# Down-sampled attention and a gated feed-forward layer in one kernel: w_out by seven products in the middle stage, in a written step order

## The chip, the core and the metric

The kernel runs on one core of one Trainium2 chip. The metric is the device time of one execution in microseconds (us). A core has TensorE (matrix products, into PSUM, eight banks of 512 float32 per partition), VectorE, ScalarE, GpSimd and SyncE. In the profile they are PE (PEld for its weight loads), DVE, ACT, POOL and SP. Each works through its own queue in order, and they wait for each other by semaphores. DMAs are issued from the queues of GpSimd, SyncE and ScalarE.

## The reference

Two layers follow each other. The first is attention over 8 batches of 8 heads, 576 positions of width 64: a coarse attention on q, k and v averaged over groups of four positions, its output repeated four times, plus a local one in which each position sees the three neighbours on either side. The second takes the result as 4608 tokens of width 512 through a gated layer of width 1536.

```python
out_d = sm_attn(q_d, k_d, v_d)                  # q, k, v averaged over 4 positions
out_up = np.repeat(out_d, factor, axis=2)
mask = np.abs(pos[:, None] - pos[None, :]) < factor
...
out_local = np.matmul(attn, v)                  # softmax inside the mask
x = (out_up + out_local) as tokens x 512
gate = np.maximum(x @ w_gate, 0.0)
val = x @ w_val
return gate * val @ w_out
```

## The kernel before

All five engines follow the order in which the program is written (`manual_schedule`); nothing is moved by a planner at build time, so the order of the calls is the order of each queue.

The attention is done by head pairs, 32 of them (`hp`), four to a batch. The feed-forward layer is done by chunks of 512 tokens, nine of them (`c`), in four slots each. Slot `s` belongs to chunk `s // 4` and works on head pair `s + 4`: the attention runs four pairs ahead. So slots 0 to 27 hold both, slots 28 to 35 hold the feed-forward layer alone (the tail), and four filling steps come before slot 0.

A slot of the middle stage (from slot 8; `emit_slot`) does this:

- `emit_h` three times: gate and value product of one 128-wide piece of the 1536, each four matmuls of 128x512 (`emit_h_mm`, line 516) into a pair of banks. ScalarE takes the relu of the gate half (line 531), VectorE multiplies it with the value half into `gT` (line 532, the "gate"). Pairs 0 and 1 (banks 0 to 3) take turns.
- `emit_y`: the w_out product of 128 tokens of the chunk before, twelve matmuls of 128x512 (line 541), a copy by ScalarE (line 549) and an output DMA from ScalarE's queue.
- `emit_s1`, written inside `emit_y` after its first two matmuls: the scores of the pair (lines 314 and 325) into banks 4 to 7, two exponentials and one for the coarse scores by ScalarE (lines 334 and 343), two mask products by VectorE (line 337).
- `emit_pool`: VectorE sums q and k of the next pair over four positions (line 234), from the transposed copy `qkT` that a transposing DMA on SP's queue (`emit_qkT`) made two slots earlier.
- `emit_s2w`: sums and denominators of the attention (lines 459 and 467), again into banks 4 to 7, a logarithm of each head's denominators (line 477), an exponential for the inverse (line 480), two products by VectorE (`xn`, line 483), and `emit_xsum` (line 442), which adds the repeated coarse part and writes `xT`, what the feed-forward products read.
- GpSimd issues the loads four pairs ahead: q and k (line 195) into `qk16`, v (line 220) into `vw`, rings of seven; v once more in another layout into `v4` (line 222), a ring of five. From this it pools v in two adds, `emit_v2` (line 280) and `emit_v1` (line 286), into `vd`, a ring of three.

The tail does w_out by units of 256 tokens (`Unit`): a 2x2 blocked product by seven products in place of eight, of six matmuls of 128x256 each (line 603). Four sums of the token side (`s1` to `s4`, line 597) and four differences of the weights (`emit_wt`, line 572, made in slots 24 to 27) are formed by VectorE. The products `p1` to `p7` accumulate into three PSUM regions `a`, `b`, `d`. Between them ScalarE copies `a` into `m1`, `m2`, `m3`, and VectorE adds these to `b` or `d` for the output blocks. In the tail `a`, `b` and `d` have a bank each.

Of the kernel before, what the change touches and what calls it, by code (L numbers as in the profile page):

```python
# [14 lines left out]
ET = mybir.EngineType  # L15

# [41 lines left out]
def kernel(  # L58
# [27 lines left out]
    VS = 8  # L86
# [23 lines left out]
    def ring(n, shape, dtype, name):  # L110
# [3 lines left out]
    NV4 = 5  # L114
# [12 lines left out]
    xo = ring(3, [96, NB + 2, 128], FP16, "xo_")  # L127
    rden = ring(2, [128, 2, 360], FP32, "rden_")
    xn = ring(2, [128, 2, 360], FP16, "xn_")
# [7 lines left out]
    wt = [  # L137
        t.rearrange("p i c -> p (i c)").rearrange("p (j d) -> p j d", d=256) for t in qkfull[0:4]
# [38 lines left out]
    def emit_load_qk(hp):  # L177
        r = hp % NL
        b, off = head_off(hp)
        for src, dst in ((q, qk16[r][:, 0, :]), (k, qk16[r][:, 1, :])):  # L180
            if hp == 0 and src is q:
                nc.sync.dma_start(
                    q32.rearrange("p (n d) -> p n d", d=64),
                    _dap(src, off, [[D, 96], [NQ * D, 2 * NB], [1, D]]),
                )
                nc.scalar.copy(out=dst, in_=q32)
            elif hp < NTP:
                nc.gpsimd.dma_start(
                    dst.rearrange("p (n d) -> p n d", d=64),
                    _dap(src, off, [[D, 96], [NQ * D, 2 * NB], [1, D]]),  # L190
                )
            else:
                dv = dst.rearrange("p (j h d) -> p j h d", h=2, d=64)
                for hh in range(2):
                    nc.gpsimd.dma_start(  # L195
                        dv[:, :, hh, :],
                        _dap(src, off + hh * S * D, [[D, 96], [NQ * D, NB], [1, D]]),
                    )

    def emit_load_v(hp):  # L200
# [18 lines left out]
        else:  # L219
            nc.gpsimd.dma_start(t, _dap(v, base, [[D, WK], [NQ * D, n], [1, D]]))  # L220
        if hp >= NVP:
# [87 lines left out]
    def emit_s1(hp, p0):  # L309
# [22 lines left out]
        for g in range(2):  # L332
            o = ee[r2][:, :, 288 * g : 288 * g + 288]
            nc.scalar.activation(  # L334
                out=o, in_=ps[0:WK, p0 + 2 * g : p0 + 2 * g + 2, 0:288], func=AF.Exp, scale=scale
            )
            nc.vector.tensor_tensor(  # L337
                out=o,
                in0=o,
                in1=_sap(masks_sb, (0, WK), 288 * g, [[0, 2], [1, 288]]),  # L340
                op=ALU.mult,
            )
        nc.scalar.activation(  # L343
            out=ed[r2][:, :, 0 : 2 * SD].rearrange("p h (c t) -> p c h t", c=2),
# [3 lines left out]
        )  # L348

# [43 lines left out]
    def emit_s2t(hp, between):  # L393
        r2 = hp % 2
        e, d = ee[r2], ed[r2]
        for g in range(2):
            for hh in range(2):
                nc.tensor.matmul(  # L398
                    out=ps[64 * hh : 64 * hh + 64, 4 + g, 0:288],
# [5 lines left out]
            for c in range(2):  # L405
                for hh in range(2):
                    nc.tensor.matmul(
                        out=ps[64 * hh : 64 * hh + 64, 4 + g, 288:360],
# [5 lines left out]
        for g in range(2):  # L414
            for j in range(3):
                for hh in range(2):
                    nc.tensor.matmul(
                        out=ps[64 * hh : 64 * hh + 64, 2 + g, NQ * j : NQ * j + NQ],
# [5 lines left out]
            for c in range(2):  # L424
                for hh in range(2):
                    nc.tensor.matmul(
                        out=ps[64 * hh : 64 * hh + 64, 2 + g, 288:360],
# [5 lines left out]
        r, x = rden[r2], xn[r2]  # L433
        nc.scalar.activation(out=r, in_=ps[:, 4:6, 0:360], func=AF.Ln)
        between()
        nc.scalar.activation(out=r, in_=r, func=AF.Exp, scale=-1.0)
        nc.vector.tensor_tensor(out=x, in0=ps[:, 2:4, 0:360], in1=r, op=ALU.mult)
        emit_xsum(hp)

    def emit_xsum(hp):  # L440
        b, kk, x = hp // NPB, hp % NPB, xn[hp % 2]
# [6 lines left out]

    def emit_s2w(hp):
        r2 = hp % 2  # L450
        vflat = vw[hp % NL].rearrange("p b c -> p (b c)")
        e, d = ee[r2], ed[r2]
        for hh in range(2):
            for g in range(2):
                bank = 4 + 2 * hh + g
                for j in range(3):
                    lo = 288 * g + NQ * j
                    v0 = 128 * (NB * hh + 3 * g + j) - 64 * hh
                    nc.tensor.matmul(  # L459
                        out=ps[:, bank, NQ * j : NQ * j + NQ],  # L460
                        lhsT=vflat[:, v0 : v0 + 128],
                        rhs=e[:, hh, lo : lo + NQ],
                        start=True,
                        stop=True,
                    )
                for c in range(2):
                    nc.tensor.matmul(  # L467
                        out=ps[:, bank, 288:360],
                        lhsT=vd[hp % 3][:, c, 64 * hh : 64 * hh + 128],
                        rhs=d[:, hh, c * SD + 72 * g : c * SD + 72 * g + 72],  # L470
                        start=(c == 0),
                        stop=(c == 1),
                    )
        r, x = rden[r2], xn[r2]
        for hh in range(2):
            lo, de = 64 * hh, 64 - 64 * hh
            nc.scalar.activation(  # L477
                out=r[lo : lo + 64], in_=ps[de : de + 64, 4 + 2 * hh : 6 + 2 * hh, 0:360], func=AF.Ln
            )
        nc.scalar.activation(out=r, in_=r, func=AF.Exp, scale=-1.0)  # L480
        for hh in range(2):
            lo = 64 * hh
            nc.vector.tensor_tensor(  # L483
                out=x[lo : lo + 64],
                in0=ps[lo : lo + 64, 4 + 2 * hh : 6 + 2 * hh, 0:360],
                in1=r[lo : lo + 64],
                op=ALU.mult,
            )
# [35 lines left out]
    def emit_h(c, jj, pp, parts=((0, range(4)), (1, range(4)))):  # L524
        h1, h2 = pair(pp)[:, 0, :], pair(pp)[:, 1, :]
# [3 lines left out]
        def gate():  # L529
            r1 = ffn.tile([128, TCH], FP16, name="r1", tag="r1")  # L530
            nc.scalar.activation(out=r1, in_=h1, func=AF.Relu)  # L531
            nc.vector.tensor_tensor(out=gT[c % 2][:, jj, :], in0=r1, in1=h2, op=ALU.mult)  # L532

        return gate
# [33 lines left out]
    def emit_wt(i):  # L568
        (b11, b12), (b21, b22) = halves
        t1, t2, t3, t4 = wt  # L570
        o, a, b = ((t1, b12, b11), (t2, b22, t1), (t3, b22, b12), (t4, b21, t2))[i]
        nc.vector.tensor_tensor(out=o, in0=a, in1=b, op=ALU.subtract)

    class Unit:


        def __init__(self, c, u, banks):
            self.c, self.u = c, u
            self.a, self.b, self.d = (ps[:, k, 0:256] for k in banks)
            self.s1, self.s2, self.s3, self.s4 = sa[u]  # L580
            self.m1, self.m2, self.m3 = sums[u]
# [19 lines left out]
        def mm(self, out, left, right, first):  # L601
            for i in range(NK):
# [3 lines left out]
                    rhs=right[:, i, :],  # L606
# [5 lines left out]
        def p1(self):  # L612
# [3 lines left out]
            self.mm(self.a, self.x[0][0], halves[0][0], True)  # L616
            nc.scalar.copy(out=self.m1, in_=self.a)

        def p2(self):
            self.mm(self.d, self.x[0][1], halves[1][0], True)  # L620
            nc.vector.tensor_tensor(out=self.y[0][:, 0:256], in0=self.d, in1=self.m1, op=ALU.add)
            self.out(0, 0)

        def p6(self):
            self.mm(self.a, self.s2, wt[1], False)
            nc.scalar.copy(out=self.m2, in_=self.a)
# [3 lines left out]

        def p7(self):
            self.mm(self.a, self.s3, wt[2], False)
            nc.scalar.copy(out=self.m3, in_=self.a)
# [3 lines left out]
        def p4(self):  # L637
            self.mm(self.a, self.x[1][1], wt[3], False)
# [223 lines left out]
```

The softmax here doesn't subtract the row's maximum and nothing guards it: scores larger than these inputs give would overflow.

## Time and profile before

| | before |
|---|---|
| median of 8 runs | 353.87 us (353.14 to 354.64) |
| profiled execution: time, span | 353.77 us, 352.0 us |
| granted TensorE clock, mean | 1.000 |
| PE, DVE, ACT, POOL busy | 345.6, 236.7, 214.6, 184.8 us |
| gate and value products (L516) | 432 + 432 matmuls, 111.5 + 111.2 us |
| w_out products by 512 (L541) | 288 matmuls, 70.1 us |
| w_out products by 256 in the tail (L603) | 13.3 + 9.3 + 4.8 + 4.7 us in four groups |
| chain that ended last | PE 93%, DVE 2%, ACT 1%, DMA 1% |

In a row of a timeline the first number is the start in us after the span's start, the second the time that the row took, then come engine, source line, operation, what is written and read with its shape, and how many instructions are merged (x2). A bracket gives the idle time of the engine before the row and what ended it. Matmuls overlap: a row of four lasts longer than the distance from its start to the next row's start, and this distance is what it takes of TensorE's time. A row of a stretch gives its bounds, its length, then the busy time of PE, PEld, DVE, ACT and POOL with instructions begun in it, the clock, the DMA share and GB/s.

### The profile page before, as it was taken

The numbers are of one execution on the slowest core, as the hardware profiler recorded it, in microseconds if no ns is written. First come the engines' busy times: TensorE is split into PE (matmuls) and PEld (weight loads), VectorE is DVE, ScalarE is ACT, GpSimd is POOL, SyncE is SP. The second block draws the span as 40 slices with busy tenths as digits, with TensorE's granted clock in tenths as the row PEclk, the third lists the DMA queues.
The fourth block names the chain that finished last, engine by engine and source line by source line (L and its number), as shares of the span: only waits on it lengthen the run. The fifth ranks groups of instructions, "written<-read, shape, count | busy, mean of one in ns | idle before, by whom it ended". The sixth has DMA issues, their size and how long they took to land.

```text
span 352.0 us, 7538 instructions
## 1 busy us (share of the span) xinstructions
PE 345.6 (98%) x2947; PEld 188.1 (53%) x2947; DVE 236.7 (67%) x397; ACT 214.6 (61%) x370; POOL 184.8 (53%) x233
## 2 busy tenths in 40 slices
PE   7999999999999999999999999999999999999996
PEld 3765555555544555555555554455555465655575
DVE  5895566586667776677777776776777655354581
ACT  3767876676667766666666667767667533333332
POOL 8986556899899976666668877722100000000000
PEclk9999999999999999999999999999999999999999
DMA  9999999999999999999999999960000000101013
GB/s 152 168 171 187 183 194 158 154 157 178 179 165 166 156 181 131 126 130 128 125 120 154 124 113 136 125 96 30 32 31 32 33 30 32 45 30 47 15 47 119
DMA packets 168770, 40.26 MB, mean 114 GB/s; under 512 B 150080, under 2 KB 165664, under 8 KB 168736
## 3 DMA queue, kind: packets, MB, share of 16 engines
q0 software_dynamic: 132960, 22.93, 86.0%
q1 hardware_dynamic: 32176, 10.55, 17.1%
q10 hardware_dynamic: 3600, 6.32, 5.3%
q8 instruction: 23, 0.38, 0.5%
q14 instruction: 11, 0.09, 0.1%
HBM read 46.45 MB, written 9.44 MB: 159 GB/s over the span
## 4 chain that ended last, share of the span: by engine, by line
PE 93%; DVE 2%; ACT 1%; DMA 1%; issue 1%; POOLq 0%
PE ps L516 52%; PE ps L541 18%; PE ps L603 8%; PE ps L459 3%; PE ps L325 2%; PE ps L314 2%; PE ps L253 2%; PE ps L467 2%; DMA qk<-in_k_dram 1%; DVE xo L386 1%; PE ps L682 1%; PE ps L398 1%; PE ps L298 0%; ACT rden L477 0%; PE ps L495 0%
## 5 line engine op out<-in xcount | busy, mean ns | idle before, releaser
L516 PE MATMUL ps<-xT,wv_sb 128*128 128x512 f16 x432 | 111.2, 379 | 0.5 <-DVE gT L532 0.5
L516 PE MATMUL ps<-xT,wg_sb 128*128 128x512 f16 x432 | 111.5, 379 | 0.1
L532 DVE TENSOR_TENSOR gT<-r,ps 128x512 f16<-128x512 f16 x108 | 72.1, 686 | 48.2 <-PE ps L516 39.9
L531 ACT ACTIVATE r<-ps 128x512 f16<-128x512 f32 x108 | 63.9, 592 | 38.5 <-PE ps L516 35.5
L483 DVE TENSOR_TENSOR xn<-ps,rden 64x720 f16<-64x720 f32 x46 | 41.6, 905 | 43.4 <-ACT rden L480 42.7
L541 PE MATMUL ps<-wo_sb,gT 128*128 128x512 f16 x288 | 70.1, 380 | 0.0
L516 PEld LDWEIGHTS <-wv_sb 128*128 128x128 f16 x432 | 42.2, 98 | 51.3 <-issue 0.8
L516 PEld LDWEIGHTS <-wg_sb 128*128 128x128 f16 x432 | 39.6, 98 | 38.7 <-DVE xT L509 0.6
L334 ACT ACTIVATE ee<-ps 112x576 f16<-112x576 f32 x64 | 38.1, 646 | 27.8 <-PE ps L325 27.3
L477 ACT ACTIVATE rden<-ps 64x720 f32<-64x720 f32 x46 | 35.2, 765 | 12.6 <-PE ps L467 12.0
L541 PEld LDWEIGHTS <-gT 128*128 128x128 f16 x288 | 26.2, 98 | 29.9
L286 POOL TENSOR_TENSOR vd<-v 72x256 f16<-72x256 f32 x23 | 17.2, 749 | 45.0 <-PE ps L467 44.6
L195 POOL DMA_DIRECT2D qk<-in_q_dram x46 | 34.0, 741 | 5.6 <-DMA wo_sb<-in_moe_w_out_dram 2.8
L195 POOL DMA_DIRECT2D qk<-in_k_dram x46 | 33.2, 728 | 2.5 <-DMA qk<-in_q_dram 1.9
L220 POOL DMA_DIRECT2D vw<-in_v_dram x30 | 28.9, 964 | 4.7 <-PE ps L253 1.8
L234 DVE TENSOR_REDUCE qkd<-qkT 128x288 f16<-128x1152 f16 x23 | 31.0, 1346 | 0.4 <-DMA qkT<-qk 0.4
L337 DVE TENSOR_TENSOR ee<-ee,cst_sb 112x576 f16<-112x576 f16 x64 | 27.0, 460 | 1.9 <-ACT ee L334 1.7
L280 POOL TENSOR_TENSOR v<-v 72x512 f32<-72x512 f16 x23 | 26.8, 1167 | 0.3
L549 ACT COPY y_sb<-ps 128x512 f32<-128x512 f32 x24 | 14.1, 586 | 17.5 <-PE ps L541 17.5
L442 DVE TENSOR_TENSOR xT<-xn 128x576 f16<-128x576 f16 x28 | 22.9, 818 | 0.2
L343 ACT ACTIVATE ed<-ps 72x576 f16<-72x576 f32 x32 | 20.5, 641 | 0.0
L459 PEld LDWEIGHTS <-vw 112*128 112x128 f16 x276 | 17.4, 97 | 5.4
(97 smaller groups left out, 381.5 us busy)
## 6 DMA issues: line engine op xcount, KB each, us to landing
out_dram<-y_sb ACTq DMA_DIRECT2D x24, 256.0 KB, 5.0
vw<-in_v_dram POOLq DMA_DIRECT2D x30, 168.0 KB, 6.0
qk<-in_q_dram POOLq DMA_DIRECT2D x46, 72.0 KB, 4.0
qk<-in_k_dram POOLq DMA_DIRECT2D x46, 72.0 KB, 3.9
v<-in_v_dram POOLq DMA_DIRECT2D x23, 144.0 KB, 6.0
out_dram<-y_sb SPq DMA_DIRECT2D x22, 128.0 KB, 1.7
wg_sb<-in_moe_w_gate_dram POOLq DMA_DIRECT2D x4, 384.0 KB, 9.9
wv_sb<-in_moe_w_val_dram POOLq DMA_DIRECT2D x4, 384.0 KB, 10.8
```

The costliest lines, as they stand in the source:

```text
L195: nc.gpsimd.dma_start(dv[:, :, hh, :], _dap(src, off + hh * S * D, [[D, 96], [NQ * D, NB], [1, D]]),)
L220: nc.gpsimd.dma_start(t, _dap(v, base, [[D, WK], [NQ * D, n], [1, D]]))
L234: nc.vector.tensor_reduce(out=qkd[hp % 2].rearrange("p i t -> p (i t)"), in_=qkT[hp % 4][:, 0 : 2 * S].rearrange("p (t f) -> p t f", f=4), ...
L334: nc.scalar.activation(out=o, in_=ps[0:WK, p0 + 2 * g : p0 + 2 * g + 2, 0:288], func=AF.Exp, scale=scale)
L459: nc.tensor.matmul(out=ps[:, bank, NQ * j : NQ * j + NQ], lhsT=vflat[:, v0 : v0 + 128], rhs=e[:, hh, lo : lo + NQ], start=True, stop=True,)
L477: nc.scalar.activation(out=r[lo : lo + 64], in_=ps[de : de + 64, 4 + 2 * hh : 6 + 2 * hh, 0:360], func=AF.Ln)
L483: nc.vector.tensor_tensor(out=x[lo : lo + 64], in0=ps[lo : lo + 64, 4 + 2 * hh : 6 + 2 * hh, 0:360], in1=r[lo : lo + 64], op=ALU.mult,)
L516: nc.tensor.matmul(out=pair(pp)[:, which, :], lhsT=w[:, kk, bass.ts(jj, 128)], rhs=xT[:, kk, c * TCH : (c + 1) * TCH], start=(kk == 0), st ...
L531: nc.scalar.activation(out=r1, in_=h1, func=AF.Relu)
L532: nc.vector.tensor_tensor(out=gT[c % 2][:, jj, :], in0=r1, in1=h2, op=ALU.mult)
L541: nc.tensor.matmul(out=y_ps, lhsT=gT[c % 2][:, jj, bass.ts(ty, 128)], rhs=wo_sb[:, jj, :], start=(jj == 0), stop=(jj == NJJ - 1),)
L603: nc.tensor.matmul(out=out, lhsT=left[:, i, :], rhs=right[:, i, :], start=(first and i == 0), stop=(i == NK - 1), skip_group_check=True,)
```

## The change

Slots 8 to 27 no longer call `emit_slot`. A written list, `ORDER`, gives every step of one chunk, and `emit_periods` runs it for chunks 2 to 6; each step is one instruction or one group on one engine, so that the list fixes each queue's order. `kind/argument/u` names a step: `u` is the half of the chunk (two slots), `a` and `b` are the head pairs of its two slots, `<` and `>` mean the chunk before and after. `hg/i` and `hv/i` are gate and value products, `relu/i` and `gate/i` what follows them, `scores`, `exp`, `mask`, `ed`, `o`, `ln`, `inv`, `xn`, `xsum` the attention of a pair (`o/a11` is the last of four pieces of its products), `p/1` to `p/7`, `keep/1` to `keep/3` and `c11` to `c22` a unit's products, copies and outputs, `sum`, `sumhi`, `next` its four sums.

`emit_y` is gone from these slots: each half of a chunk has a unit for 256 tokens of the chunk before. The unit shares PSUM banks 0 to 3 with the gate and value products (the one pair that the half does not use for its even pieces); `b` and `d` share one bank. Its outputs go out from SP's queue, 128 rows of 512 at once. The four weight differences get buffers of their own (one lies in the part of `xT` that chunk 0 has used) and are made in slots 4 to 6, and the token sums use the space of `xo`. `rden` and `xn` fall from two buffers to one, `v4` from five to three. Slot 7 runs the list `LEAD_IN`. The v pools change places with the loads in GpSimd's queue from slot 7 on. The tail keeps its form; its first unit's sums are partly formed ahead.

```diff
+ORDER = """
+p/1/0 gate/5/1< scores/a/0 keep/1/0 gate/4/1< hg/0/0 exp/a0/0 sumhi/0/0 sumhi/1/0 exp/a1/0
+hv/0/0 mask/a0/0 ed/a/0 mask/a1/0 p/2/0 next/0/1< relu/0/0 next/1/1< o/a00/0 o/a01/0 c11//0
+o/a10/0 ln/a0/0 o/a11/0 sum/2/0 p/6/0 v/a/1 sum/3/0 p/5/0 keep/2/0 pool/b/0 v2/b/0 ln/a1/0 p/7/0
+hg/2/0 keep/3/0 v1/a/1 inv/a/0 c22//0 p/4/0 gate/0/0 v2/a/0 p/3/0 xn/a1/0 c21//0 relu/2/0 hg/1/0
+xn/a0/0 qk/a0/1 hv/2/0 relu/1/0 qk/a1/1 c12//0 xsum/a/0 scores/b/0 qk/a2/1 next/0/0 hv/1/0
+exp/b0/0 v/b/0 exp/b1/0 hg/4/0 mask/b0/0 gate/1/0 v4/a/1 ed/b/0 hg/3/0 mask/b1/0 relu/4/0
+gate/2/0 v1/b/0 o/b00/0 o/b01/0 o/b10/0 pool/a/0 ln/b0/0 o/b11/0 hv/4/0 v2/a/1 ln/b1/0 hv/3/0
+gate/4/0 inv/b/0 v4/b/1 next/1/0 p/1/1 relu/3/0 xn/b1/0 v4/b/0 p/2/1 keep/1/1 qk/a3/1 hg/5/0
+xn/b0/0 qk/b0/1 p/6/1 gate/3/0 relu/5/0 qk/b1/1 scores/a/1 next/2/0 keep/2/1 next/3/0 hg/0/1
+v/b/1 exp/a1/1 exp/a0/1 hv/5/0 mask/a1/1 qk/b2/1 ed/a/1 mask/a0/1 p/7/1 qk/b3/1 c11//1 gate/5/0
+o/a00/1 keep/3/1 o/a01/1 o/a10/1 pool/b/1 ln/a0/1 o/a11/1 p/5/1 qk/a0/0> ln/a1/1 p/4/1 v/a/0>
+c22//1 inv/a/1 hv/0/1 xsum/b/0 qk/a1/0> c21//1 xn/a0/1 p/3/1 relu/0/1 v2/b/1 hg/1/1 xn/a1/1
+hg/2/1 relu/1/1 qk/a2/0> xsum/a/1 scores/b/1 c12//1 qk/a3/0> relu/2/1 gate/0/1 hg/3/1 exp/b1/1
+v4/a/0> exp/b0/1 hv/1/1 mask/b1/1 ed/b/1 mask/b0/1 hv/2/1 gate/1/1 relu/3/1 pool/a/1 o/b00/1
+o/b01/1 o/b10/1 ln/b0/1 o/b11/1 hv/3/1 qk/b0/0> gate/2/1 ln/b1/1 qk/b1/0> hg/5/1 gate/3/1
+inv/b/1 v1/a/0> hv/4/1 relu/5/1 xn/b0/1 v1/b/1 hg/4/1 qk/b2/0> xn/b1/1 hv/5/1 relu/4/1 qk/b3/0>
+xsum/b/1
+"""
...
-    VS = 8
+    VS = 7
...
-    NV4 = 5
+    NV4 = 3
+    PS = 8
...
-    rden = ring(2, [128, 2, 360], FP32, "rden_")
-    xn = ring(2, [128, 2, 360], FP16, "xn_")
+    rden = keep.tile([128, 2, 360], FP32, name="rden")
+    xn = keep.tile([128, 2, 360], FP16, name="xn")
+    wtnew = ring(3, [128, NK, 256], FP16, "wt_")
...
+    def slot_unit(s):
+        c, u = s // 4 - 1, s % 4 // 2
+        if s >= NP - LEAD:
+            return tail_unit(c, u)
+        k = 2 * (((s - PS) // 2 + 1) % 2)
+        return Unit(c, u, ((k, 0), (k + 1, 0), (k + 1, 256)), sx, sums[0], False)
...
+    PAIR_STEPS = {
...
+        "pool": pool_ab,
+        "v1": lambda hp, a: emit_v1(hp + 1),
+        "v2": lambda hp, a: emit_v2(hp + 2),
+        "qk": ahead(emit_load_q1),
+        "v": ahead(emit_load_v),
+        "v4": ahead(emit_load_v4),
+    }
+
+    def emit_periods(c0, c1):
+        for base in range(c0 - 2, c1 + 2):
+            for tok in ORDER.split():
+                c = base + {">": 1, "<": -1}.get(tok[-1], 0)
+                kind, arg, u = tok.rstrip("<>").split("/")
+                if c0 <= c < c1 or c == c0 - 1 and f"{kind}/{arg}/{u}" in LATE:
+                    emit_step(kind, arg, int(u), c)
...
             emit_h(c, jj, 0)()
-            if 24 <= s < 28:
-                emit_wt(s - 24)
-            if hp < NP:
-                emit_s2w(hp)
+            emit_wt(s - 3)
+            emit_s2w(hp)
...
-        for s in range(NP - LEAD):
+        for s in range(PS):
             gate = emit_slot(s, gate)
+        emit_periods(PS // 4, (NP - LEAD) // 4)
```

## The prediction

> **What bounds the kernel now.** I read the page's first two parts first, then the timeline of TensorE over one slot of the middle stage, then the timeline of VectorE over the same stage, then the stretches of one slot each, and last the places where VectorE and GpSimd overlap. "Slot" is one head pair's step; slots 8 to 27 are 20 equal ones.
>
> ```profile
> PE 345.6 (98%) x2947; PEld 188.1 (53%) x2947; DVE 236.7 (67%) x397; ACT 214.6 (61%) x370; POOL 184.8 (53%) x233
> ...
> 86.47 0.59 PE L541 MATMUL ps<-wo_sb,gT 128*128 128x512 f16 x2
> 86.99 0.25 PE L314 MATMUL ps<-qkd 64*72 64x144 f16 x2
> ...
> 87.50 2.33 PE L541 MATMUL ps<-wo_sb,gT 128*128 128x512 f16 x10
> 89.66 1.03 PE L516 MATMUL ps<-xT,wg_sb 128*128 128x512 f16 x4
> 90.53 1.03 PE L516 MATMUL ps<-xT,wv_sb 128*128 128x512 f16 x4
> 91.39 0.29 PE L459 MATMUL ps<-ee,vw 112*128 112x96 f16 x3
> ...
> 92.18 1.03 PE L516 MATMUL ps<-xT,wg_sb 128*128 128x512 f16 x4
> ...
> 95.63 0.59 PE L541 MATMUL ps<-wo_sb,gT 128*128 128x512 f16 x2
> ```
>
> TensorE never rests: a slot repeats after 95.63 - 86.47 = 9.16 us. From start to start, ten w_out matmuls take 2.16 us (0.216 each), a group of four gate or value matmuls 0.865, the scores 0.6 with their two borders, the attention products 0.79. The seven-product scheme already runs in the tail, and gives its price:
>
> ```profile
> 322.03 0.82 PE L603 MATMUL ps<-wo_sb,vw 128*128 128x256 f16 x6
> 322.69 1.03 PE L516 MATMUL ps<-xT,wg_sb 128*128 128x512 f16 x4
> ```
>
> A product of six 256-wide matmuls takes 0.66 us of the line, its result is there 0.16 us later. VectorE in one slot:
>
> ```profile
> 167.71 1.84 DVE L483 TENSOR_TENSOR xn<-ps,rden 64x720 f16<-64x720 f32 x2 [2.06 <-ACT rden L480]
> 169.59 1.28 DVE L532 TENSOR_TENSOR gT<-r,ps 128x512 f16<-128x512 f16 x2
> 170.79 0.75 DVE L442 TENSOR_TENSOR xT<-xn 128x576 f16<-128x576 f16 x1
> 171.46 0.82 DVE L337 TENSOR_TENSOR ee<-ee,cst_sb 112x576 f16<-112x576 f16 x2
> 172.19 1.35 DVE L234 TENSOR_REDUCE qkd<-qkT 128x288 f16<-128x1152 f16 x1
> 174.13 0.69 DVE L532 TENSOR_TENSOR gT<-r,ps 128x512 f16<-128x512 f16 x1 [0.59 <-PE ps L516]
> ```
>
> It is busy 6.5 of 9.16 us, and its 2.65 us of rest are what the change spends.
>
> **The change part by part.** A chunk is four slots; five chunks change (slots 8 to 27).
>
> TensorE. Out go 48 w_out matmuls a chunk, 48 x 0.216 = 10.37 us; in come 14 products of 0.655 (twelve matmuls in the tail take 1.31), 9.17 us. That is 1.2 us a chunk, 35.5 instead of 36.66. Nothing else on TensorE is added; the attention products are only cut into four pieces. Five chunks: 6.0 us, and no more can be had.
>
> VectorE. Each unit (256 tokens, two slots) adds four sums and three combining adds. In the tail four sums run from 281.42 to 283.42, 2.0 us; two adds in a row start 0.33 us apart. A chunk: 2 x (2.0 + 3 x 0.33) = 6.0, and 0.3 for two sums that are cut in two: 6.3 us, or 1.6 a slot. VectorE then has 6.5 + 1.6 = 8.1 us of work in a slot of 8.87, 91%. It fits, but a lost microsecond in a slot is no longer free.
>
> ScalarE. Two 0.586 us copies a unit become four of 0.37: +0.16 us a slot on 6.32 busy. It loses the issue of the output (0.34 us a slot, its own queue), which moves to SP. Cost nothing; its cover is 2.4 us of rest a slot.
>
> SP. Its queue gets two outputs a unit between the transposes. Each waits for the last copy of its rows, at most some 3 us, and the transposes behind it wait too. A transpose is read two slots (17.7 us) after its issue and lands in 5.8 us, so some 9 us cover that. Nothing.
>
> GpSimd's work is the same by count (16 q/k issues of 0.74 us, eight v issues of 0.95 or 0.74, four pools of 1.10 and four of 0.67 a chunk: 26 of 35.5 us); only its order changes and the v4 ring falls from five to three. The v4 loads wait for a pool that stands several steps earlier in the same queue. Their own landing (6.0 us) is covered by more than a slot. Nothing for lateness.
>
> Slots 4 to 7. Four weight differences of 0.95 us leave slots 24 to 27, where they lay in the 2.06 us before `xn`; in slots 5 and 6 they lie in the same gap, in slot 4 behind `xT`. Zero on both sides, and if that gap were not there each would delay the scores by at most 0.95. Slot 7 gets the same matmuls in another order; its masks (done at 172.28 in the slot shown) are ready before the attention products even when these start 0.86 us earlier. Zero, with 1 us as the upper end.
>
> Waits. I laid the written order of one chunk end to end with these durations, TensorE without a gap. Every step that it waits for is ready, but narrowly in places. p6, p5, p7: p7 overwrites what `keep/2` copies. 0.16 + 0.04 + 0.37 us after p6, and about 0.06 for the semaphore, against 0.655 of p5: 0.03 to spare. p4, p3, hg/1: the same sum, the same margin. p6 waits for the sum `next/1`, 0.2 to spare. Since the sums b and d share one PSUM bank, p5 waits for c11, p3 for c22 and hv/1 for c12, each 0.4 to 0.6 to spare. Behind each stands all of TensorE. Bounds: 0 (margins hold) to 0.4 us a chunk (each relay 0.1 late); I take 0.1, 0.5 in all.
>
> The lock. Here a row speaks against the change. When GpSimd adds, a VectorE instruction with both inputs in SBUF runs late, or makes GpSimd late:
>
> ```profile
> 248.26 1.31 POOL L286 TENSOR_TENSOR vd<-v 72x256 f16<-72x256 f32 x1 [7.33 <-PE ps L467]
> ...
> 248.04 0.95 DVE L572 TENSOR_TENSOR qk<-wo_sb 128x1536 f16<-128x1536 f16 x1
> ...
> 108.04 0.74 POOL L286 TENSOR_TENSOR vd<-v 72x256 f16<-72x256 f32 x1
> ...
> 107.75 1.35 DVE L337 TENSOR_TENSOR ee<-ee,cst_sb 112x576 f16<-112x576 f16 x2
> ```
>
> The pool that met the weight difference took 1.31 us instead of 0.72; the mask pair that met a pool took 1.35 instead of 0.82. Gates beside pools stay at 0.69, since they read PSUM. The Trainium skill, "SBUF — State Buffer", section "Who interferes with whom", says why: with two SBUF inputs VectorE reads through the port pair that it shares with GpSimd, and whoever is first holds it for the whole instruction. By the rule a VectorE instruction can lose a full pool, 1.10 us, and two in a row 1.77; the rows show 0.42 to 0.54 a hit. Before, from about 130 us on, GpSimd stands at a wait for TensorE each slot and its pools fall beside gates, so no hit is left; between 105.5 and 133 us, when it runs free, hits cost VectorE about 0.6 us a slot:
>
> ```profile
> 105.50:114.60 9.10, 9.10 (x76) 4.59 (x74) 7.28 (x9) 6.32 (x10) 9.06 (x12) 1.00 1.70 166
> ...
> 142.10:151.30 9.20, 9.20 (x78) 4.69 (x76) 6.49 (x10) 6.32 (x10) 6.42 (x9) 1.00 1.18 128
> ```
>
> TensorE did not feel it, having 2.65 us of cover. The change raises such instructions from 12 to 22 a chunk (masks 8, `xsum` 4, sums 10). And GpSimd is bound to the order at one wait: the pool `v1/a/1` waits for o/a11 of slot a, since the vd ring has three places. From there 0.67 + 1.10 + 3 x 0.74 + 0.95 + 0.74 = 5.7 us later come `v1/b/0` and `v2/a/1`, 1.77 us of lock; VectorE has `xsum/a`, `next/0`, and both masks of pair b there, from 5.8 to 8.7 us after the same point. o/b01 needs the second mask at 9.3: 0.5 to spare. Lost to the lock: 0 (the pools fall elsewhere) to 1.77 less 0.5 = 1.3 us a chunk. I take the middle, 0.7: more than one hit of the rows (0.5, hidden by the spare), less than two whole pools. Chunk 6 has no loads, so its pools come earlier, beside `xn`: four chunks, 2.8 us.
>
> Sum: -6.0 + 0.5 + 2.8 = -2.7 us. The profiled execution took 353.77 (span 352.0, 1.8 around it), 0.1 under the median of the runs; so 351.1 to 351.2, and I say 351.2.
>
> **The rivals.** *The order holds.* Pools fall beside gates, `xn` and the reduction, as they do before from 130 us on; only the narrow relays cost 0.5: 348.4. For it: every other wait has cover, and that stage before was free of hits. Against it: GpSimd needs 26 of 35.5 us, so it is early everywhere but at its wait, wherever its steps are written.
>
> *The lock takes more than is saved.* One mechanism: DVE instructions and pools alternate, so that masks of pair b lose both pools in each chunk, and the masks of the next pair lose `v2/b/1` too, which comes 16 us after the same wait, where those masks stand. 1.3 + 0.9 us a chunk in four chunks = 8.8, with 0.5: +3.3, 357. It decides from 1.2 us of stall a chunk on. For it: VectorE at 91% doesn't catch up before its next due step. Against it: a stall of TensorE moves the later masks, not GpSimd, and so moves them out of the way.
>
> *Washed out.* 1.0 to 1.2 us a chunk lost: within 0.7 us of before.
>
> That the change doesn't save TensorE time is excluded: the tail row gives 0.66 for a product in this very form.
>
> **How the numbers follow.** A difference under 0.2% (0.7 us) is what a measurement here can't tell from none. Some of the lock felt (-1 to -4): 0.42. The order holds (-4.5 to -6): 0.24. Washed out: 0.12. More lost than saved: 0.22. Faster 0.66, same 0.12, slower 0.22. The range goes from 348.2 (the order holds, relays 0.3) to 355.6, half way into the slower case; about 2 in 10 lie outside. The likeliest case alone is 349.8 to 352.9.
>
> **What would show it.** Products at 0.66 from start to start, and chunks of 35.5 us plus stalls, from TensorE's starts. If I am right, gaps of TensorE before the attention products behind a mask, with that mask at 0.8 us or more beside a pool, and VectorE some 0.5 to 1 us a slot busier than 8.1. If gaps stand instead before p7 or hg/1 behind copies, the relays were mis-sized. If chunks are 35.5 and masks 0.45, the order holds. A gap behind a transpose or a v load would prove my zero for SP or GpSimd wrong.

## The result, and the profile after

| | before | after |
|---|---|---|
| median of the runs | 353.49 us (352.87 to 354.99, 32 runs) | 349.91 us (349.10 to 352.04, 11 runs) |
| profiled execution: time, span | 353.77, 352.0 us | 349.10, 347.3 us |
| slot 4's scores to the end of the span | 291.02 us | 286.05 us |

The ratio is 0.9904 with an interval of 0.9886 to 0.9922: the kernel is 3.4 us faster, 3.6 by the two medians (forecast: 2.7). The third line of the table is the one that I compare kernels by below. The scores of slot 4 begin at 60.98 us before and at 61.25 after; among all profiles of this study they begin between 60.00 and 63.01, in kernels whose steps up to there are nearly the same. The difference is there by 25 us, after TensorE's wait for the first q/k loads, and stays constant from there on. Differences between two profiled spans hold it, differences of this line don't.

The page of the changed kernel, its first two parts and two groups:

```profile
PE 339.9 (98%) x3127; PEld 205.4 (59%) x3127; DVE 273.6 (79%) x479; ACT 214.4 (62%) x390; POOL 190.1 (55%) x233
DVE  4896556787899999999999999999989745354481
...
L327 POOL TENSOR_TENSOR vd<-v 72x256 f16<-72x256 f32 x23 | 21.7, 955 | 27.6 <-PE ps L526 27.0
L382 DVE TENSOR_TENSOR ee<-ee,cst_sb 112x576 f16<-112x576 f16 x64 | 31.3, 511 | 3.6 <-ACT ee L376 2.8
```

TensorE is still the engine that never rests, with 5.7 us less work. VectorE has 37 us more, and the row of tenths shows where: it is at 9 through the whole middle. The last two rows are the lock in the mean. In the kernel before, the same two groups are:

```profile
L286 POOL TENSOR_TENSOR vd<-v 72x256 f16<-72x256 f32 x23 | 17.2, 749 | 45.0 <-PE ps L467 44.6
L337 DVE TENSOR_TENSOR ee<-ee,cst_sb 112x576 f16<-112x576 f16 x64 | 27.0, 460 | 1.9 <-ACT ee L334 1.7
```

The pool `v1` took 749 ns and now takes 955, a mask 460 and now 511.

TensorE in one slot of chunk 4, in the timeline:

```profile
172.14 0.82 PE L684 MATMUL ps<-wt,xo 128*128 128x256 f16 x6
172.80 0.82 PE L684 MATMUL ps<-xT,xo 128*128 128x256 f16 x6
173.45 0.82 PE L684 MATMUL ps<-wt,xo 128*128 128x256 f16 x6
174.11 1.03 PE L588 MATMUL ps<-xT,wg_sb 128*128 128x512 f16 x4
```

A product takes 0.655 us from start to start, as in the tail of before, and p/6, p/5, p/7 follow one another without a gap. How long a chunk takes is read from the rows in which its first scores begin (chunks 2, 3 and 4; the next are at 203.93 and 239.56):

```profile
96.65 0.25 PE L355 MATMUL ps<-qkd 64*72 64x144 f16 x2
...
133.00 0.25 PE L355 MATMUL ps<-qkd 64*72 64x144 f16 x2
...
168.46 0.25 PE L355 MATMUL ps<-qkd 64*72 64x144 f16 x2
```

Chunks 2 to 5 took 36.35, 35.46, 35.47 and 35.63 us; before, each took 36.65. So two chunks run at TensorE's pace, chunk 5 lost 0.16, and the first is 0.88 longer (0.13 of it, as e1_no_pools will show, without any lock). Slots 4 to 7 took 35.40 against 35.18: in the written order a product of 0.655 us stands ahead of the next scores and not two w_out matmuls of 0.216, so they begin 0.22 later and nothing is lost by it. All engines over chunk 3 (PE, PEld, DVE, ACT, POOL):

```profile
132.79:168.26 35.47, 35.47 (x327) 22.07 (x324) 33.57 (x53) 25.23 (x44) 28.01 (x34) 1.00 1.69 145
```

VectorE is busy 33.57 of 35.47 us, 95%, where I had worked out 91% ahead of any lock.

Now the stall of the first chunk (all engines, timeline):

```profile
99.80 1.35 DVE L678 TENSOR_TENSOR xo<-xo,gT 128x640 f16<-128x640 f16 x1
...
100.04 0.74 POOL L327 TENSOR_TENSOR vd<-v 72x256 f16<-72x256 f32 x1
...
101.20 0.83 PE L684 MATMUL ps<-wt,xo 128*128 128x256 f16 x6 [0.58 <-DVE xo L678]
```

The sum `next/1` ran beside the pool `v1` and took 1.35 us instead of 0.49. p/6 needs it: TensorE is idle for 0.58 by its row, and p/6 starts 0.75 later in its chunk than it does in a chunk without a stall. It is the lock that I had forecast, at a sum instead of a mask, and nearly all of it in the first of the four chunks over which I had spread it. Where I had put it, at the masks of pair b, stands this (chunk 3; the same in chunks 4 and 5):

```profile
143.74 0.75 DVE L382 TENSOR_TENSOR ee<-ee,cst_sb 112x576 f16<-112x576 f16 x1 [0.15 <-ACT ee L376]
...
143.03 1.14 POOL L327 TENSOR_TENSOR vd<-v 72x256 f16<-72x256 f32 x1
...
144.25 1.25 POOL L321 TENSOR_TENSOR v<-v 72x512 f32<-72x512 f16 x1
...
145.01 0.81 DVE L382 TENSOR_TENSOR ee<-ee,cst_sb 112x576 f16<-112x576 f16 x1
...
145.74 0.29 PE L518 MATMUL ps<-ee,vw 112*128 112x96 f16 x3
...
145.94 0.29 PE L518 MATMUL ps<-ee,vw 112*128 112x96 f16 x3
```

Both masks are hit by exactly the pools that I named, `v1/b/0` and `v2/a/1`, and take 0.75 and 0.81 us instead of 0.45. TensorE's rows behind them have no idle time: the second mask ends at 145.82, and the products that read it, o/b01, are the second piece, at 145.94. The spare holds, with 0.12 us left.

The 0.16 us of chunk 5 are the lock too, at another instruction, `xsum`, which takes 0.75 us when nothing meets it:

```profile
227.04 1.44 DVE L504 TENSOR_TENSOR xT<-xn 128x576 f16<-128x576 f16 x1
...
230.46 1.02 DVE L504 TENSOR_TENSOR xT<-xn 128x576 f16<-128x576 f16 x1
231.51 0.42 DVE L725 TENSOR_TENSOR y_sb<-ps,q 128x256 f32<-128x256 f32 x1
...
231.99 1.89 PE L588 MATMUL ps<-xT,wv_sb 128*128 128x512 f16 x8
```

Each of the two `xsum` began beside a pool `v2` (at 226.72 and 229.71). They made c12 (231.51) late, and the value product whose bank c12 reads started 0.06 us after its end, 0.17 late.

So there are two theories to tell apart. *Lock:* what the changed kernel lacks to TensorE's pace, and the scatter of that from execution to execution, is the lock between VectorE and GpSimd, felt because the sums have filled VectorE. *Rivals:* the relays `keep`, p/7 and hg/1 wait for copies; or loads and transposes come late in GpSimd's new order.

### The profile page after: what moved, and what is told of

The parts are those of the page before. It is cut to its first block, busy times and chain, and to the rows that moved or that the text cites. A ratio compares the mean times of both kernels' runs of the same rounds, so it can differ in the third digit from the quotient of the medians.

```text
span 347.3 us, 7968 instructions
## 1 busy us (share of the span) xinstructions
PE 339.9 (98%) x3127; PEld 205.4 (59%) x3127; DVE 273.6 (79%) x479; ACT 214.4 (62%) x390; POOL 190.1 (55%) x233
## 5 line engine op out<-in xcount | busy, mean ns | idle before, releaser
L588 PE MATMUL ps<-xT,wg_sb 128*128 128x512 f16 x432 | 110.0, 380 | 0.1
L588 PE MATMUL ps<-xT,wv_sb 128*128 128x512 f16 x432 | 109.6, 379 | 0.5 <-DVE gT L609 0.4
L588 PEld LDWEIGHTS <-wv_sb 128*128 128x128 f16 x432 | 41.0, 98 | 47.1 <-issue 1.3
L327 POOL TENSOR_TENSOR vd<-v 72x256 f16<-72x256 f32 x23 | 21.7, 955 | 27.6 <-PE ps L526 27.0
L684 PEld LDWEIGHTS <-gT 128*128 128x128 f16 x288 | 28.2, 98 | 10.3
L382 DVE TENSOR_TENSOR ee<-ee,cst_sb 112x576 f16<-112x576 f16 x64 | 31.3, 511 | 3.6 <-ACT ee L376 2.8
L718 ACT COPY q<-ps 128x256 f32<-128x256 f32 x39 | 14.5, 371 | 21.0 <-PE ps L684 20.7
L684 PEld LDWEIGHTS <-xo 128*128 128x128 f16 x240 | 22.8, 98 | 6.4 <-DVE xo L678 0.7
L684 PE MATMUL ps<-wo_sb,gT 128*128 128x256 f16 x192 | 24.9, 273 | 0.0
```

The source lines that it names most:

```text
L382: nc.vector.tensor_tensor(out=o, in0=o, in1=_sap(masks_sb, (0, WK), 288 * g, [[0, 2], [1, 288]]), op=ALU.mult,)
L588: nc.tensor.matmul(out=pair(pp)[:, which, :], lhsT=w[:, kk, bass.ts(jj, 128)], rhs=xT[:, kk, c * TCH : (c + 1) * TCH], start=(kk == 0), st ...
L684: nc.tensor.matmul(out=out, lhsT=left[:, i, :], rhs=right[i], start=(first and i == 0), stop=(i == NK - 1), skip_group_check=True,)
```

## The experiments

All ratios are to the kernel before, on the same chip. "From slot 4" is the line of the table above, for the profiled execution.

| run | median us (range, runs) | ratio, interval | from slot 4 |
|---|---|---|---|
| after | 349.91 (349.10 to 352.04, 11) | 0.9904 [0.9886, 0.9922] | 286.05 |
| e0_again | 350.69 (349.11 to 353.90, 9) | 0.9921 [0.9893, 0.9949] | 287.06 |
| e1_no_pools | 348.88 (348.67 to 349.18, 4) | 0.9868 [0.9856, 0.9881] | 285.17 |
| e2_eighth | 357.03 (355.36 to 357.40, 6) | 1.0092 [1.0074, 1.0109] | 292.01 |
| e3_loads_as_before | 352.55 (350.74 to 354.62, 22) | 0.9979 [0.9965, 0.9993] | 289.05 |
| e4_pools_later | 350.60 (349.52 to 351.71, 6) | 0.9915 [0.9896, 0.9935] | 288.54 |
| e5_no_sums | 348.87 (348.31 to 351.00, 6) | 0.9891 [0.9868, 0.9913] | 285.80 |
| e6_first_pool_early | 350.25 (348.92 to 352.45, 6) | 0.9918 [0.9893, 0.9942] | 287.59 |
| e7_before_no_pools | 353.21 (352.83 to 354.95, 14) | 1.0001 [0.9988, 1.0014] | 291.00 |
| e8_vw6 | 349.85 (348.30 to 350.34, 6) | 0.9890 [0.9869, 0.9912] | 287.98 |
| e9_vw6_first | 349.13 (348.62 to 350.44, 6) | 0.9890 [0.9872, 0.9908] | 285.29 |

**The changed kernel again, unedited (e0_again).** No edit: it gives the changed kernel its own scatter on the chip of the first experiments, and a second profile.

> The changed kernel once more, unedited, for a second profiled execution and more times. Theory T1 (TensorE sets the chunk; the lock between VectorE and GpSimd is felt only where it eats more than the spare): ratio to before 0.990, chunks of 35.5 us, one gap of 0.5 to 0.8 us in the first chunk of the written order before p/6, and the masks of pair b at 0.7 to 0.8 us each beside the pools without a gap of TensorE behind them. Theory T2 (VectorE, 94% busy in these chunks, sets them): chunk lengths vary with VectorE's busy time from chunk to chunk.

It had 350.69 us, and its profile lost 1.01 us more from slot 4 on than the first one. Its first chunk took 37.39 us. By the starts of its products, TensorE lost 0.14 before the first value product, 0.83 before p/6, as above, and 0.51 behind the masks of pair b, the place of my forecast:

```profile
107.70 2.41 POOL L321 TENSOR_TENSOR v<-v 72x512 f32<-72x512 f16 x1
...
109.26 1.18 DVE L382 TENSOR_TENSOR ee<-ee,cst_sb 112x576 f16<-112x576 f16 x1 [0.15 <-ACT ee L376]
...
110.95 0.94 DVE L382 TENSOR_TENSOR ee<-ee,cst_sb 112x576 f16<-112x576 f16 x1
...
111.95 0.29 PE L518 MATMUL ps<-ee,vw 112*128 112x96 f16 x3 [0.33 <-DVE ee L382]
```

The pool took 2.41 us instead of 1.15 and the first mask 1.18; the gate behind it started late too, and so the second mask, and the products had to wait. Another 0.45 us went in the last slot of the chunk, in two places behind an `xsum` (125.04, beside the pool at 124.83) of 1.58 us instead of 0.75 and a mask pair of 1.35 instead of 0.82. Later chunks had 35.47 to 35.53. Two executions of one kernel thus lose 0.9 and 1.9 us, nearly all of it in the first chunk.

**No v pools from slot 8 on (e1_no_pools).** In `emit_periods`:

```diff
                 kind, arg, u = tok.rstrip("<>").split("/")
+                if kind in ("v1", "v2"):
+                    continue
```

> Leaves out GpSimd's v pools in slots 8 to 27 (the coarse attention there reads stale v averages), all else as in the changed kernel. No GpSimd addition is left to hold the port. T1: the masks fall to 0.41 us each, the sum before p/6 in the first chunk to 0.48, its gap of 0.65 us goes and the one of 0.17 in the fourth; the profile is 0.8 us shorter than the changed kernel's 349.1 (348.3), and the runs spread less. T2: VectorE gets 0.6 to 1 us a chunk back and every chunk becomes shorter than 35.47, 3 us or more in all. Third view (the lock was never felt): no difference from the changed kernel.

It took 348.88 us. From scores to scores chunks 2 to 5 took 35.60, 35.47, 35.47 and 35.46. The only delay on TensorE in the five chunks is 0.13 before the first value product, which comes behind a gate that follows the late `xsum` of slot 7; the changed kernel has it as well. The window of chunk 3 (PE, PEld, DVE, ACT, POOL):

```profile
132.79:168.26 35.47, 35.47 (x326) 22.11 (x324) 32.47 (x53) 25.25 (x44) 20.43 (x27) 1.00 1.55 153
```

In the first chunk p/6 starts at 101.05 directly behind the attention products, where the changed kernel stood. The masks have a mean of 469 ns. This parts the theories: every copy, relay, load and transpose of the change is still there, and TensorE waits for none of them. The pools cost 1.0 us by the median of the changed kernel, 1.8 by that of e0_again; by the profiles from slot 4 on 0.88 and 1.89. It is also the measure of TensorE's term: 285.17 against 291.02, 5.85 us.

**An eighth product in each unit (e2_eighth).**

```diff
         def p2(self):
-            self.mm(self.d, self.x[0][1], half_js[1][0], True)
+            for _ in range(1 if self.split else 2):
+                self.mm(self.d, self.x[0][1], half_js[1][0], True)
```

> Each unit in slots 8 to 27 does product p2 twice over (the second overwrites the first with the same numbers), so that eight products of six matmuls are done and TensorE has as much w_out work as before, in the written order and with all the sums. T1: ten products of 0.655 us come on top, +6.5 us on the changed kernel, minus what their cover gives back (at most 0.8): 355 to 356.4, that is 1.5 to 2.5 us above the kernel before. T2 (VectorE sets the chunk): much less than 6.5 us, since VectorE's work is unchanged: 350 to 353. If the written order itself were the gain: below before, 348 to 351.

357.03 us, and later chunks 36.77 to 36.78 instead of 35.47: 1.31 for two products, 0.654 each. Ten of them are 6.54, and by the medians it is 6.3 above e0_again, 7.1 above the changed kernel. In the later chunks nothing of the extra time is absorbed, so TensorE's work is the whole pace of the chunks; in the first, the longer pace left 0.3 us to the lock instead of 0.75. With eight products the scheme is 0.9% slower than before; all of the gain hangs on the product that is saved.

**Four GpSimd steps later (e4_pools_later).** `v1/b/0`, `v2/a/1`, `v4/b/1` and `v4/b/0` go from around the masks and products of pair b to where the next scores begin:

```diff
-gate/2/0 v1/b/0 o/b00/0 o/b01/0 o/b10/0 pool/a/0 ln/b0/0 o/b11/0 hv/4/0 v2/a/1 ln/b1/0 hv/3/0
...
+xn/b1/0 p/2/1 keep/1/1 qk/a3/1 hg/5/0 xn/b0/0 qk/b0/1 p/6/1 gate/3/0 relu/5/0 qk/b1/1 v1/b/0
+v2/a/1 v4/b/1 v4/b/0 scores/a/1 next/2/0 keep/2/1 next/3/0 hg/0/1 v/b/1 exp/a1/1 exp/a0/1 hv/5/0
```

> In the written order the pools v1/b/0 and v2/a/1 with the two v4 loads behind them stand after three more q/k issues, 2.2 us later in GpSimd's queue, so that they fall beside the reduction and the gates instead of beside the masks of pair b. T1: these masks fall from 0.75 and 0.81 us to 0.41 to 0.45, VectorE gets 0.6 us a chunk back, and the time stays (within 0.3 us of the changed kernel), since those hits were covered. If those hits were felt in most executions: 1 to 2 us faster than the changed kernel's median, 348 to 349.

350.60 us, the same as e0_again. The masks are hit no less (mean 521 ns), and the losses stand at other places: 0.53 before the attention products at 119.81, 0.36 before p/6 at 138.39, 0.68 before p/3 at 142.56. A step of GpSimd's list is not a point in time: between its waits GpSimd runs as fast as it can, and its pools come whenever the steps ahead of them are done. This profile showed one thing more, in slot 5, where the edit has no part:

```profile
74.06 1.35 DVE L274 TENSOR_REDUCE qkd<-qkT 128x288 f16<-128x1152 f16 x1 [1.64 <-DMA qkT<-qk]
...
75.92 1.82 DVE L650 TENSOR_TENSOR wt<-wo_sb 128x1536 f16<-128x1536 f16 x1
77.66 1.83 DVE L544 TENSOR_TENSOR xn<-ps,rden 64x720 f16<-64x720 f32 x2
...
78.61 0.25 PE L354 MATMUL ps<-qkd 64*72 64x144 f16 x2 [0.43 <-DVE xn L544]
```

VectorE waited 1.64 us for a transpose, the weight difference behind it met a pool (1.82 us instead of 0.95), and `xn` came behind both. The gap ahead of `xn`, which was to hide the difference, had been eaten by the transpose.

**GpSimd's order as before (e3_loads_as_before).** All GpSimd steps go ahead of each slot's scores, in the order of before: `v1`, four `qk`, `v2`, `v`, `v4`.

```diff
+p/1/0 gate/5/1< v1/a/0 qk/a0/0 qk/a1/0 qk/a2/0 qk/a3/0 v2/a/0 v/a/0 v4/a/0 scores/a/0 keep/1/0
...
+c21//0 relu/2/0 hg/1/0 xn/a0/0 hv/2/0 relu/1/0 c12//0 xsum/a/0 v1/b/0 qk/b0/0 qk/b1/0 qk/b2/0
+qk/b3/0 v2/b/0 v/b/0 v4/b/0 scores/b/0 next/0/0 hv/1/0 exp/b0/0 exp/b1/0 hg/4/0 mask/b0/0 gate/1/0
```

> Undoes one part: in slots 8 to 27 GpSimd's queue has the kernel before's order again (per slot v1, four q/k issues, v2, v, v4), all other queues as in the changed kernel. T1 (the lock is felt where pools meet sums or masks with little spare, above all in the first chunk of the written order): the first v1 then runs near 95 us beside xn instead of 100 us beside the sum that p/6 waits for, so that this gap of 0.65 to 0.75 us goes; in later chunks v2 falls beside xn or xsum; 0 to 1 us faster than the changed kernel's median 350.7, with gaps at other places. If loading and pooling earlier is itself a gain: 1 us or more slower, with waits of TensorE behind GpSimd or a DMA.

352.55 us: 1.9 above e0_again, which ran on another chip (2.0 by the two ratios), and most of the gain gone. Its first chunk took 37.57 us and chunks 3 and 4 36.07, 0.6 above TensorE's pace. In the first chunk:

```profile
100.52 0.74 POOL L326 TENSOR_TENSOR vd<-v 72x256 f16<-72x256 f32 x1
...
100.66 0.96 DVE L677 TENSOR_TENSOR xo<-xo,gT 128x640 f16<-128x640 f16 x1
...
101.68 0.50 PE L683 MATMUL ps<-wt,xo 128*128 128x256 f16 x3 [0.66 <-DVE xo L677]
```

The victim is `next/1` again (0.96 us instead of 0.49, beside `v1`), and 1.4 us earlier TensorE had waited 0.45 for a mask pair of 1.35 us, beside two DMA issues of GpSimd. So GpSimd's new order is not a zero, as I had it: without it 1.9 of the 2.8 us are gone. These gaps are behind VectorE and not behind a load. Chunks 3 to 5 each lose 0.36 before p/6: there the `xsum` ahead of the chunk's first scores begins 0.17 to 0.19 us after the pool `v2` and takes 1.60 to 1.63 us instead of 0.75, and VectorE is late from there on.

**No sums from slot 8 on (e5_no_sums).** The unit's sums are left out, the pools stay:

```diff
         def sums(self, lo=0, hi=NK, which=range(4)):
+            if not self.split:
+                return
```

> Leaves out the ten token sums a chunk in slots 8 to 27 (the products there read zeros), with GpSimd's pools left in. It takes 4.3 us a chunk from VectorE and the sums from the lock. T1: pools still lengthen masks and xsum, but VectorE is 81% busy and TensorE has no gap behind them: 348.6 to 349.2, as without the pools (348.9), and a narrow spread. If it is the pools' part in GpSimd's queue (late loads) and not the lock, the gaps stay: 350 to 351.

348.87 us. The window of chunk 3 with the sums gone:

```profile
132.79:168.26 35.47, 35.47 (x326) 22.12 (x324) 29.41 (x44) 25.23 (x44) 26.77 (x32) 1.00 1.66 139
```

The masks are still hit (mean 494 ns), and the five chunks still have no gap (35.46 to 35.47). With VectorE at 29.41 of 35.47 us, 83%, a hit is taken up before the next due step. Its one loss, 0.8 us, lies in slots 6 and 7. So it takes both, the pools and the sums: neither alone stops TensorE from slot 8 on. That VectorE had cover before is e7_before_no_pools.

**The kernel before without v pools from slot 8 on (e7_before_no_pools).**

```diff
         else:
-            emit_v1(hp + 1)
-            emit_in(hp + 4, lambda: emit_v2(hp + 2))
+            emit_in(hp + 4)
```

> The kernel before with GpSimd's v pools left out from slot 8 on (the coarse attention reads stale v averages there). T1: TensorE has no gap in slots 8 to 27 before either, since VectorE has 2.65 us of rest a slot, so nothing is to be had: within 0.5 us of the kernel before. If the pools cost something in themselves (GpSimd's time, the loads behind them): 1 us or more faster, as the changed kernel became without them.

A ratio of 1.0001: before, the lock cost nothing that these runs can show (its interval is 0.5 us to either side). Its range is that of the kernel before (352.83 to 354.95 against 352.86 to 355.26 on that chip), so the scatter of before is not the lock; the start of the program, 60.00 against 60.98 us at slot 4's scores in the two profiles, is of that size.

**The first pool of the chunks earlier (e6_first_pool_early).** `v1/a/0` of chunk 2, the pool in the first chunk's stall, is put ahead of all steps of slot 8:

```diff
     def emit_periods(c0, c1):
+        emit_step("v1", "a", 0, c0)
...
+                if (kind, arg, u, c) == ("v1", "a", "0", c0):
+                    continue
```

> One GpSimd instruction is moved: the first v1 of the written order (pair 13) is issued six DMA issues (some 5 us) earlier, near 95 us beside xn, and no longer meets the sum that p/6 of the first chunk waits for. T1: the gap of 0.65 to 0.75 us near 100 us goes, the others stay: 0.7 us faster than the changed kernel's median (350.7), 350.0 or a little less, if nothing else moves. If that gap has another cause: no change.

The first chunk's stall went, as meant (35.61 us), but 350.25 is no gain: chunks 3 and 5 took 36.82 and 36.50. In chunk 5:

```profile
210.37 0.72 POOL L327 TENSOR_TENSOR vd<-v 72x256 f16<-72x256 f32 x1 [4.16 <-PE ps L526]
210.47 1.04 DVE L678 TENSOR_TENSOR xo<-gT 128x768 f16<-128x768 f16 x1
...
211.06 1.47 POOL L321 TENSOR_TENSOR v<-v 72x512 f32<-72x512 f16 x1
...
211.43 1.50 DVE L678 TENSOR_TENSOR xo<-gT,xo 128x768 f16<-128x768 f16 x1
...
214.59 0.60 PE L684 MATMUL ps<-wo_sb,xo 128*128 128x256 f16 x4 [0.66 <-DVE y_sb L733]
```

This is a race. TensorE's o/a11 releases GpSimd for `v1/a/1`, at the time when VectorE comes to `sum/2` and `sum/3`. Here GpSimd was 0.1 us ahead: the sums took 1.04 and 1.50 us instead of 0.55 each, the reduction behind them and c22 were late, and p/3 waited 0.66. VectorE came late because it had been hit once already, 5 us before:

```profile
205.42 1.42 DVE L504 TENSOR_TENSOR xT<-xn 128x576 f16<-128x576 f16 x1
```

This `xsum` began beside a pool (205.05, 1.16 us) and took 0.67 us too long; p/6 was 0.21 late by it. In the changed kernel's profile VectorE was ahead in chunk 3 (`sum/2` at 136.52, and then):

```profile
136.99 0.55 DVE L678 TENSOR_TENSOR xo<-gT,xo 128x768 f16<-128x768 f16 x1
136.99 1.13 POOL L327 TENSOR_TENSOR vd<-v 72x256 f16<-72x256 f32 x1 [2.75 <-PE ps L526]
```

Both sums kept 0.55 us and the pool paid. VectorE has only 0.47 us in hand there, and the written order doesn't protect it. The race was lost twice more, in chunk 3 of this run and in chunk 3 of e4_pools_later (a sum of 1.50 us in both), and both times the `xsum` before the chunk's scores had run long, 1.47 and 1.63 us, here beside load issues of GpSimd and the start of a pool. In all three chunks p/6 and p/3 together came 1.03 to 1.04 us late.

**GpSimd's wait at the load instead of the pool (e8_vw6, e9_vw6_first).** The ring `vw` is used with six places instead of seven, so that the load `v/a/1`, ahead of the pools in GpSimd's queue, is what waits for TensorE. e9 has the edit of e6 as well.

```diff
+    NVW = 6
...
     def emit_load_v(hp):
-        r = hp % NL
+        r = hp % NVW
```

> The v ring vw is used with six places in place of seven, so that GpSimd's load v/a/1 waits for o/a11 of slot a, which holds its whole queue back by some 2 us in each half chunk once it has caught up with TensorE. The pools then fall at 5.8 to 8.6, 12.5 to 14.3, 24.5 to 25.6 and 29.3 to 30.7 us of a chunk, beside the reduction, gates and xn, where the written order puts them, and not beside the sums before p/7 and p/3 nor the masks of pair b. T1 (what is lost is lock hits, and who wins the race between v1/a/1 and these sums differs from run to run): later chunks lose their hits, masks of pair b at 0.41 to 0.45, no gap of TensorE after the first chunk, the runs spread less, median 349.6 to 350.2 (the first chunk's stall stays). If later loads matter: slower than 350.7, with TensorE behind a v load.

> e8's ring of six together with the earlier first v1 of the run e6_first_pool_early. T1: neither the first chunk's gap near 100 us nor those of later chunks: 349.0 to 349.6, near the 348.9 of the run without pools, and the best correct version. If e6's gaps near 141 and 213 us came from its one moved instruction and not from the race, they stay: 350.2.

In e9, chunk 3:

```profile
136.42 0.55 DVE L679 TENSOR_TENSOR xo<-gT,xo 128x768 f16<-128x768 f16 x1
136.59 0.94 POOL L259 DMA_DIRECT2D vw<-in_v_dram  x1 [4.94 <-PE ps L527]
...
144.34 0.45 DVE L383 TENSOR_TENSOR ee<-ee,cst_sb 112x576 f16<-112x576 f16 x1
144.43 0.94 POOL L328 TENSOR_TENSOR vd<-v 72x256 f16<-72x256 f32 x1
```

The wait ends with the issue of a load, the sums pass with 0.55 us, the next pool (at 137.54) falls beside the reduction, and the masks of pair b keep 0.46 and 0.45 us: `v1/b/0` now begins when the second of them is nearly done. From slot 4 on e9 takes 285.29 us, 0.1 above the kernel without pools. By its median, 349.13, it is the best version that computes everything, but its interval overlaps that of the changed kernel, and I don't claim the 0.8 us between their medians. e8's profile lost 1.9 us in slots 4 to 7 and 0.74 in chunk 2, and nothing but 0.1 behind: it orders the chunks once GpSimd stands at its wait, and not the slots before that.

## Why the prediction was right, and where it was not

*TensorE's term, -6.0.* Right from slot 4 on. The kernel without pools gives -5.85 there, a chunk at its pace 35.47 instead of 36.65, and a further product costs its 0.654.

*The relays, +0.5.* Wrong, though small: zero. The margins of 0.03 us that I had laid out hold, and in e1_no_pools, where nothing else disturbs, no product waits for a copy. The lower bound was the right one.

*The lock, +2.8.* The mechanism, the pair of pools, and the masks that they hit are as forecast. The term is mis-sized: 1.0 to 1.8 us by the medians. And it is composed otherwise. I wrote 0.7 us for each of four chunks, with the spare of 0.5 us used up. At the masks of chunks 3 to 5 a hit took 0.3 and 0.36 us, the spare holds that, and TensorE felt nothing; it felt 0.17 once, behind two `xsum`. In the first chunk, where GpSimd is still behind with its loads and doesn't yet stand waiting for o/a11, pools meet `next/1`, masks and an `xsum` and cost 0.75 us in the one profile and 1.8 in the other. I had spread the cost evenly and missed that this chunk carries it. To this comes the race at o/a11, which isn't in the prediction at all: 1.0 us for each chunk in which VectorE loses it. The 0.42 to 0.54 us a hit that the prediction gives come from `xsum` rows that it doesn't print (1.17 to 1.29 us instead of 0.75); the two rows that it prints give 0.59 and 0.53.

*The sum.* -6.0 + 0.5 + 2.8 was -2.7. Measured in the profiles it is -5.85 + 0.88, with 0.27 of a later start: -4.7. The medians give -3.4 to -3.6, and the lock isn't all of the difference. e1_no_pools, which has no lock from slot 8 on, is 4.6 us below the kernel before by the medians (its four runs lie within 0.51 us), 1.2 less than its profile gives from slot 4 on; e5_no_sums and e9 fall short in the same way (4.4 against 5.2, 4.1 against 5.7). So about 1 us is lost ahead of slot 4, or in executions of which there is no profile. The prediction has no term for it, and its cause stays open. The forecast is 1.3 us above the median because the two terms that I added are both too large. That it came so near is partly luck: without the loss that nobody forecast it would have been about 2.5 us off.

*GpSimd's new order, zero.* This step failed. I had argued that GpSimd is early everywhere but at its wait, wherever its steps are written. e4_pools_later bears that out for four steps, e3_loads_as_before contradicts it for the whole list: 1.9 us, behind sums, masks and `xsum` that meet pools. For lateness of the loads zero was right, since no gap in the chunks stands behind a load; the order counted for the lock.

*Slots 4 to 7, zero.* It holds in the profile of the changed kernel, in e0_again, e1, e2, e6 and e9 (35.40 us each, 0.22 of it slot 7's order). It doesn't hold in e4 and e5 (1.25 and 0.8 lost, part of it behind a late transpose with a weight difference before `xn`), nor in e8 (1.9, from an `xsum` of 2.32 us and masks beside pools). My upper end was 0.95 for a difference, and I had not thought of a late load that uses up the same gap. Whether the kernel before would have lost as much behind the same transposes was not tried.

*SP, ScalarE, zero.* No gap stands behind them in the chunks.

*VectorE's load, 91%.* Right: without pools a chunk has 32.47 of 35.47 us, 91.5%. The lock adds 1.1 us to it.

*The rule on the lock.* The Trainium skill, "SBUF — State Buffer", section "SBUF: two separate sides", has the later of the two blocked until the first one's instruction is done. In the rows of chunk 3 the masks began 0.43 and 0.49 us before their pools ended and took 0.30 and 0.36 longer; in e3_loads_as_before the `xsum` of chunks 3 to 5 began 0.97 to 0.99 us before its pool ended and took 0.85 to 0.88 longer. That is a little less than the rule would make of it, and less than the whole pool that I had taken as the most that a hit can cost. The first chunk's row speaks against it: by the records (GpSimd's spans are rough) `next/1` began 0.24 us before `v1`, and yet it is the sum that lost 0.86 us, while the pool kept 0.74.

## What to carry to other kernels

When a change trades work of the bounding engine for work of another one, look at what is left of the second engine's rest, and then at who shares a port with it: hits that cost nothing at 70% busy are felt at 95%. One hit can bring on the next: an `xsum` that took 0.67 us too long made VectorE late for a meeting 5 us further on. A queue that runs free between its waits isn't scheduled by the place of its steps alone; choose what it waits at, so that the release starts a step that did no harm (here a load) instead of the one that collides. And compare profiles from a common point behind the start-up, since start-up alone differed by 3 us.

## What was not expected of the hardware

A GpSimd pool of 1.15 us was drawn out to 2.41 while three VectorE instructions ran beside it (e0_again, 107.70), and an `xsum` of 0.75 to 2.32 (e8). VectorE's instructions of two SBUF inputs also ran long beside GpSimd's DMA issues alone. In e1_no_pools, in slot 7:

```profile
88.90 1.49 POOL L233 DMA_DIRECT2D qk<-in_q_dram  x2
...
89.17 1.53 DVE L504 TENSOR_TENSOR xT<-xn 128x576 f16<-128x576 f16 x1
```

No pool runs there, and `xsum` took 1.53 us instead of 0.75. The changed kernel has a mask pair of 1.36 us instead of 0.82 at 196.27, also with load issues alone beside it. In most places the same pair does no harm; what decides it these runs don't settle. It may be why the masks of e1_no_pools stay at 469 ns and not at 450, but that is only argued.
